# A 2-D Fourier filter with a gated MLP on one core: transposes fetched one round ahead, the spectral products cut into chunks, loads in another order

## The chip, the cores and the metric

The kernel runs on one core of a Trainium2 chip. The metric is the device time of one execution in microseconds (us), median of several runs. The core's engines work side by side, each through its own queue in order: PE (TensorE, matrix products into PSUM), DVE (VectorE), ACT (ScalarE), POOL (GpSimd) and SP (SyncE). SP and ACT also issue the DMA transfers. PSUM has eight banks, and each tile in it takes a whole one here.

## The reference, cut to what matters

```
xn = layernorm(A_x)                              # 2048 x 576
X  = rfft2(xn);  s = irfft2(X * (w_r + 1j*w_i))  # branch A, 2048 x 289 spectrum
z  = gelu(xn @ w_in)                             # branch B, 2048 x 4608
z1 = z[..., :2304];  z2 = layernorm(z[..., 2304:])
g  = silu(((w_sp @ z2 + b_sp) * z1) @ w_out)
return A_x + s * g
```

## The kernel before

Tokens lie in 16 blocks of 128 partitions. The work has these stages.

**Phase 0** (lines 170 to 203) loads x in four pieces, and for each block does the layer norm on DVE and ACT and five transposes on PE. Each transpose goes to one of two PSUM buffers (pool `p0ps`); DVE (L200) and ACT (L202) in turn copy it out into `xnT`.

**The loads** (L247 to L263) are issued in turn on SP and ACT: `WIN2` (weights of branch B), the filter weights `A_w_r` and `A_w_i`, then constants: `CDSD` (first Fourier step), `GA` (second), `M16`, `TW`, `H`, `CINV`. All but `WIN2` land in memory that phase 0 holds until its end.

**Two generators** are then interleaved step by step. `pb1_gen` computes the second half of branch B: products (L481), gelu in five operations (L267 to L276), statistics (L486). `pa_gen` is branch A: first step (L285, copies L289 and L291), second step (L297 to L303), transposes of the filter (L324), then

- *stage B* (L337 to L356): 37 rounds, called `lq`. A round has two transposes into a pool of two buffers (L338), their copies to `tt` (L340, L342), two products each into `pxr` and `pxi` (L345 to L348; one buffer each), and their copies (L349, L350) to the spectrum `Xv`;
- *the filter product* (L359 to L364): six DVE operations over all 4736 columns;
- *stage IB* (L371 to L376): 10 chunks of 512 columns (the last 128), four products and two copies each;
- *the twiddle* (L385 to L390): again six DVE operations over 4736 columns;
- *stage IC* (L398 to L412): 37 rounds built as in stage B, with `dtt`, `pvr`, `pvi`;
- *stage VT* (L431 to L444): 96 transposes through two buffers, copied by L434 and L436, and after each 16 a strided copy (L442, L444), six in all;
- *stage I2* (L457 to L466): the last inverse step, written out to memory.

When `pb1_gen` has ended, the rest of `pa_gen` runs alone. After it the big part of branch B (L543 to L576) and the output (L585 to L608) follow; they use the memory that branch A gives back.

`nc.any` leaves the engine of a copy to a scheduler, which also sets the order of the instructions on each engine by priority and its own estimates. So the order is read from the built program. The large buffers are shared: G0, G1 and the two halves of G23 each hold several of the arrays in turn.

Of the kernel before, what the change touches and what calls it, by code (L numbers as in the profile page):

```python
# [103 lines left out]
def kernel(  # L104
# [173 lines left out]
    def pa_gen():  # L278
        with tc.tile_pool(name="psA", bufs=2, space=bass.MemoryType.PSUM) as psA, \
                tc.tile_pool(name="psA2", bufs=1, space=bass.MemoryType.PSUM) as psA2:  # L280
            for s2 in range(MT):
# [47 lines left out]
                if lq % 10 == 9:  # L329
                    yield  # L330
        yield
        with tc.tile_pool(name="psB", bufs=2, space=bass.MemoryType.PSUM) as psB, \
                tc.tile_pool(name="psB2", bufs=1, space=bass.MemoryType.PSUM) as psB2:
            for lq in range(LQ):
                tt = pas.tile([P, 2, P], BF16, tag="tt")
                for c in range(2):
                    pt = psB.tile([P, P], BF16, tag="tr")  # L337
# [1 line left out]
                    if c == 0:
                        nc.any.tensor_copy(out=tt[:, c, :], in_=pt[:])  # L340
                    else:
                        nc.any.tensor_copy(out=tt[:, c, :], in_=pt[:])  # L342
# [17 lines left out]
        nc.vector.tensor_tensor(out=T2, in0=Xf[:, 1, :], in1=Wf[:, 1, :], op=ALU.mult)  # L360
        nc.vector.tensor_tensor(out=CXv[:, 0, :], in0=T1, in1=T2, op=ALU.subtract)
        nc.vector.tensor_tensor(out=T1, in0=Xf[:, 0, :], in1=Wf[:, 1, :], op=ALU.mult)
        nc.vector.tensor_tensor(out=T2, in0=Xf[:, 1, :], in1=Wf[:, 0, :], op=ALU.mult)
        nc.vector.tensor_tensor(out=CXv[:, 1, :], in0=T1, in1=T2, op=ALU.add)  # L364
        yield
        with tc.tile_pool(name="psIB", bufs=2, space=bass.MemoryType.PSUM) as psIB:
            ch = [(o_, min(512, FD - o_)) for o_ in range(0, FD, 512)]
            for ci, (c0, cs) in enumerate(ch):
                pdr = psIB.tile([P, 512], F32, tag="dr")
                pdi = psIB.tile([P, 512], F32, tag="di")  # L370
                nc.tensor.matmul(pdr[:, 0:cs], lhsT=M16[:, 0, :], rhs=CXv[:, 0, c0:c0 + cs], start=True, stop=False)  # L371
                nc.tensor.matmul(pdr[:, 0:cs], lhsT=M16[:, 2, :], rhs=CXv[:, 1, c0:c0 + cs], start=False, stop=True)
                nc.tensor.matmul(pdi[:, 0:cs], lhsT=M16[:, 0, :], rhs=CXv[:, 1, c0:c0 + cs], start=True, stop=False)
                nc.tensor.matmul(pdi[:, 0:cs], lhsT=M16[:, 1, :], rhs=CXv[:, 0, c0:c0 + cs], start=False, stop=True)
# [5 lines left out]
        DD3 = G2.rearrange("p (c a k) -> p c a k", c=2, a=LQ)  # L380
        twc = TW[:, 0, :, :].to_broadcast((P, LQ, P))
        tws = TW[:, 1, :, :].to_broadcast((P, LQ, P))
        U1 = G1[:, 0:FD].rearrange("p (a k) -> p a k", a=LQ)
        U2 = G1[:, FD:2 * FD].rearrange("p (a k) -> p a k", a=LQ)
        nc.vector.tensor_tensor(out=U1, in0=DD3[:, 0, :, :], in1=twc, op=ALU.mult)  # L385
        nc.vector.tensor_tensor(out=U2, in0=DD3[:, 1, :, :], in1=tws, op=ALU.mult)
        nc.vector.tensor_tensor(out=Ev[:, 0, :, :], in0=U1, in1=U2, op=ALU.subtract)
        nc.vector.tensor_tensor(out=U1, in0=DD3[:, 0, :, :], in1=tws, op=ALU.mult)
        nc.vector.tensor_tensor(out=U2, in0=DD3[:, 1, :, :], in1=twc, op=ALU.mult)
        nc.vector.tensor_tensor(out=Ev[:, 1, :, :], in0=U1, in1=U2, op=ALU.add)  # L390
        yield
        with tc.tile_pool(name="psIC", bufs=2, space=bass.MemoryType.PSUM) as psIC, \
                tc.tile_pool(name="psIC2", bufs=1, space=bass.MemoryType.PSUM) as psIC2:
            for lq in range(LQ):
                dtt = pas.tile([P, 2, P], BF16, tag="dt")
                for c in range(2):
                    pt = psIC.tile([P, P], BF16, tag="tr")
                    nc.tensor.transpose(pt[:], Ev[:, c, lq, :], ident[:])  # L398
                    if c == 0:
                        nc.any.tensor_copy(out=dtt[:, c, :], in_=pt[:])  # L400
                    else:
                        nc.any.tensor_copy(out=dtt[:, c, :], in_=pt[:])
# [237 lines left out]
```

## Time and profile before

| | us |
|---|---|
| median of 6 runs (787.08 to 789.89) | 788.0 |
| the profiled execution | 787.72 |
| its span, first to last instruction | 785.6 |
| PE, DVE, ACT busy | 668.3, 520.5, 336.6 |

The span is 2.1 us shorter than the time of the same execution. Busy shares are means over stages that have different limits, so the profile is best read stage by stage: first the busy time of each engine in each stretch, then what each waits for there. PEclk is the granted clock of TensorE: 1.00 is the level of 2.4 GHz, 0.50 that of 1.2 GHz.

### The profile page before, as it was taken

What the parts mean: (1) busy time and instruction counts of PE and PEld (TensorE: products, weight loads), DVE (VectorE), ACT (ScalarE), POOL (GpSimd) and SP (SyncE); (2) the same over time, 40 slices, a digit from 0 to 9 for tenths busy, and PEclk for the clock granted to TensorE, in tenths of its full rate; (3) what the DMA queues carried; (4) which work ended last, traced back from release to release, by engine and by line L of the source; (5) the groups of instructions that cost most, each with busy time, mean ns of one, the idle gap of its engine ahead of it and who ended that gap; (6) DMA issues with size and microseconds to landing.
All of it is one profiled execution on the core that took longest, in us unless ns stands there. A gap on an engine that the chain in (4) does not pass through costs nothing.

```text
span 785.6 us, 10455 instructions
## 1 busy us (share of the span) xinstructions
PE 668.3 (85%) x3580; PEld 340.4 (43%) x3638; DVE 520.5 (66%) x1499; ACT 336.6 (43%) x891; POOL 15.8 (2%) x32
## 2 busy tenths in 40 slices
PE   2549998787892389687999999999999999989997
PEld 1215664343560156334444444444444444434553
DVE  6756999899738932321797777777777777652232
ACT  3435788787871267764322222222222222212322
POOL 2000000000000011000000000000000000000000
PEclk9988999898655755569899999999999999998999
DMA  7081111111399000003421211111111111015332
GB/s 256 0 297 62 61 62 61 60 61 61 93 189 207 1 1 2 0 31 123 94 47 36 54 43 34 36 39 36 37 35 35 35 35 28 1 49 185 107 92 68
DMA packets 104309, 54.07 MB, mean 69 GB/s; under 512 B 84096, under 2 KB 101120, under 8 KB 104128
## 3 DMA queue, kind: packets, MB, share of 16 engines
q10 hardware_dynamic: 61008, 28.54, 12.8%
q1 hardware_dynamic: 43248, 24.86, 11.7%
q8 instruction: 28, 0.46, 0.2%
q14 instruction: 25, 0.20, 0.1%
HBM read 30.85 MB, written 14.16 MB: 57 GB/s over the span
## 4 chain that ended last, share of the span: by engine, by line
PE 68%; DVE 15%; ACT 9%; DMA 5%; issue 3%; ACTq 0%; DVEq 0%
PE pg L567 32%; PE ph L557 10%; PE py L596 9%; PE ph L481 3%; PE py L457 3%; DVE stats L486 3%; DMA CDSD<-c_cdsd 2%; PE pt L197 2%; DVE zrow L276 2%; DVE x2t L269 2%; DVE ut L273 2%; ACT sg L275 2%; PE pt L431 2%; ACT G L434 2%; PE pvr L406 1%
## 5 line engine op out<-in xcount | busy, mean ns | idle before, releaser
L567 PE MATMUL pg<-WSPT,z2t 128*128 128x512 bf16 x1127 | 252.4, 379 | 1.4
L267 ACT ACTIVATE hs<-ph 128x512 bf16<-128x512 f32 (+1 forms) x152 | 86.0, 576 | 208.4 <-PE ph L557 183.5
L567 PEld LDWEIGHTS <-z2t 128*128 128x128 bf16 x1152 | 112.7, 98 | 135.9
L275 ACT ACTIVATE sg<-ut 128x512 bf16<-128x512 bf16 (+1 forms) x152 | 90.1, 607 | 57.1 <-DVE ut L273 34.1
L481 PE MATMUL ph<-WIN,xnT 128*128 128x512 bf16 (+1 forms) x387 | 95.8, 382 | 5.3 <-ACT hs L267 3.5
L557 PE MATMUL ph<-xnT,wb 128*128 128x512 bf16 x355 | 84.6, 387 | 4.9 <-DMA wb<-in_B_w_in_dram 4.7
L269 DVE TENSOR_TENSOR x2t<-hs 128x512 bf16<-128x512 bf16 (+1 forms) x152 | 60.1, 400 | 41.5 <-ACT hs L267 41.3
L573 DVE TENSOR_TENSOR BUF<-pg,z1T 128x512 bf16<-128x512 f32 x72 | 49.4, 687 | 44.5 <-PE pg L567 43.7
L596 PE MATMUL py<-WOUT,BUF 128*128 128x512 bf16 (+1 forms) x566 | 73.3, 290 | 4.6 <-DMA WOUT<-in_B_w_out_dram 4.0
L550 DVE TENSOR_SCALAR z2t<-z2t,RSTD,NMR 128x128 bf16<-128x128 bf16 x288 | 73.9, 311 | 2.3 <-DMA z2t<-z2n_d 1.9
L273 DVE TENSOR_TENSOR ut<-x2t,hs 128x512 bf16<-128x512 bf16 (+1 forms) x152 | 59.6, 402 | 0.2
L481 PEld LDWEIGHTS <-xnT 128*128 128x128 bf16 x400 | 40.0, 103 | 43.5 <-issue 17.0
L557 PEld LDWEIGHTS <-wb 128*128 128x128 bf16 x360 | 35.7, 99 | 48.8 <-issue 7.6
L596 PEld LDWEIGHTS <-BUF 128*128 128x128 bf16 x576 | 37.5, 99 | 40.7 <-issue 8.0
L486 DVE BATCH_NORM_STATS2 stats<-zrow 128x6 f32<-128x384 bf16 x96 | 49.0, 546 | 0.1
L602 DVE TENSOR_TENSOR g<-hx,sgm 128x576 bf16<-128x576 bf16 x16 | 7.3, 458 | 56.0 <-ACT sgm L600 44.2
L599 ACT ACTIVATE hx<-py 128x512 bf16<-128x512 f32 (+1 forms) x32 | 13.2, 414 | 67.6 <-PE py L596 67.6
L270 DVE TENSOR_SCALAR x2t<-x2t 128x512 bf16<-128x512 bf16 (+1 forms) x152 | 40.6, 278 | 1.0
L197 PE MATMUL pt<-ident,xn 128*128 128x128 bf16 (+1 forms) x80 | 17.9, 281 | 22.9 <-DVE xn L192 10.6
L276 DVE TENSOR_TENSOR zrow<-hs,sg 128x512 bf16<-128x512 bf16 (+1 forms) x80 | 30.0, 388 | 5.3 <-ACT sg L275 5.1
L285 PE MATMUL pf<-CDSD,xnT 128*128 128x296 bf16 x160 | 23.7, 293 | 11.2 <-DMA CDSD<-c_cdsd 9.8
L276 DVE TENSOR_TENSOR z1T<-hs,sg 128x512 bf16<-128x512 bf16 x72 | 30.0, 418 | 1.9 <-ACT sg L275 1.5
(133 smaller groups left out, 727.5 us busy)
## 6 DMA issues: line engine op xcount, KB each, us to landing
z2t<-z2n_d ACTq DMA_DIRECT2D x18, 512.0 KB, 4.0
z2n_d<-zrow ACTq DMA_DIRECT2D x8, 576.0 KB, 2.8
z2n_d<-zrow SPq DMA_DIRECT2D x8, 576.0 KB, 2.8
sspec_d<-srow ACTq DMA_DIRECT2D x16, 144.0 KB, 1.8
wb<-in_B_w_in_dram ACTq DMA_DIRECT2D x72, 32.0 KB, 1.9
GA<-c_ga SPq DMA_DIRECT2D x1, 1536.0 KB, 13.6
WOUT<-in_B_w_out_dram SPq DMA_DIRECT2D x9, 144.0 KB, 3.6
WOUT<-in_B_w_out_dram ACTq DMA_DIRECT2D x9, 144.0 KB, 4.1
```

Of the source, the lines that this page charges most:

```text
L267: nc.scalar.activation(out=hs[:, 0:nsz], in_=ph[:, 0:nsz], func=ACT.Identity)
L269: nc.vector.tensor_tensor(out=x2t[:, 0:nsz], in0=hs[:, 0:nsz], in1=hs[:, 0:nsz], op=ALU.mult)
L273: nc.vector.tensor_tensor(out=ut[:, 0:nsz], in0=x2t[:, 0:nsz], in1=hs[:, 0:nsz], op=ALU.mult)
L275: nc.scalar.activation(out=sg[:, 0:nsz], in_=ut[:, 0:nsz], func=ACT.Sigmoid, scale=GELU_S2)
L276: nc.vector.tensor_tensor(out=dst, in0=hs[:, 0:nsz], in1=sg[:, 0:nsz], op=ALU.mult)
L481: nc.tensor.matmul(ph[:, 0:nsz], lhsT=xnT[:, ks, m * P:(m + 1) * P], rhs=WIN2[:, ks, f0:f0 + nsz], start=(ks == 0), stop=(ks == DKS - 1))
L486: nc.vector.bn_stats(out=stats2[:, ci, :], in_=zrow[:, c0:c0 + cs])
L550: nc.vector.tensor_scalar(out=z2t[:, m, :], in0=z2t[:, m, :], scalar1=RSTD2[:, m, :], scalar2=NMR2[:, m, :], op0=ALU.mult, op1=ALU.add)
L557: nc.tensor.matmul(ph[:, 0:nsz], lhsT=wb[:, ks, :], rhs=xnT[:, ks, nb * 512: nb * 512 + nsz], start=(ks == 0), stop=(ks == DKS - 1))
L567: nc.tensor.matmul(pg[:, 0:nsz], lhsT=z2t[:, ks, :], rhs=WSPT[:, ks, nb * 512: nb * 512 + nsz], start=(ks == 0), stop=(ks == MT - 1))
L573: nc.vector.tensor_tensor(out=dst, in0=pg[:, 0:nsz].rearrange("p (a u) -> p a u", u=P), in1=z1T[:, nb * 512: nb * 512 + nsz].rearrange("p ...
L596: nc.tensor.matmul(py[:, 0:dn], lhsT=BUF[:, m, fi * P:(fi + 1) * P], rhs=WOUT[:, fi, d0:d0 + dn], start=(fi == 0), stop=(fi == FT - 1))
```

## The change

- **Phase 0:** four PSUM buffers for the transposes in place of two, and x in eight pieces in place of four.
- **Loads:** in the text, `CDSD` and `GA` come ahead of `WIN2`; the filter weights come last.
- **First step:** for the first six blocks both copies are put on ACT; the others are left to the scheduler.
- **Stages B and IC:** the transposes of the next round are written ahead of the products of this one, and the transposes' pool has three buffers in place of two.
- **Filter product and twiddle:** each is cut into the 10 chunks. All chunks of the filter product are written ahead of stage IB; the twiddle of a chunk follows the products of that chunk.
- **Stage VT:** four buffers in place of two.

```diff
-            tc.tile_pool(name="p0ps", bufs=2, space=bass.MemoryType.PSUM) as p0ps:
+            tc.tile_pool(name="p0ps", bufs=4, space=bass.MemoryType.PSUM) as p0ps:
...
-        mchunk = max(1, MT // 4)
+        mchunk = max(1, MT // 8)
...
-    for ks in range(DKS):
-        kw = kws[ks]
-        dq().dma_start(out=WIN2[0:kw, ks, :], in_=B_w_in[ks * P: ks * P + kw, Fh:F])
-    dq().dma_start(out=WNv[:, 0, :, 0:Df], in_=A_w_r.rearrange("(k2 k1) l -> k1 k2 l", k1=P))
-    dq().dma_start(out=WNv[:, 1, :, 0:Df], in_=A_w_i.rearrange("(k2 k1) l -> k1 k2 l", k1=P))
...
     dq().dma_start(out=GA[:], in_=cd_ga.ap().rearrange("p (s c k) -> p s c k", s=MT, c=3))
+    for ks in range(DKS):
+        kw = kws[ks]
+        dq().dma_start(out=WIN2[0:kw, ks, :], in_=B_w_in[ks * P: ks * P + kw, Fh:F])
...
     dq().dma_start(out=CINV[:], in_=cd_cinv.ap().rearrange("p (a c d) -> p a c d", a=LCH, c=2))
+    dq().dma_start(out=WNv[:, 0, :, 0:Df], in_=A_w_r.rearrange("(k2 k1) l -> k1 k2 l", k1=P))
+    dq().dma_start(out=WNv[:, 1, :, 0:Df], in_=A_w_i.rearrange("(k2 k1) l -> k1 k2 l", k1=P))
...
-                    if c == 0:
-                        nc.any.tensor_copy(out=Av[:, s2, c, :], in_=pf[:])
+                    if s2 < 6:
+                        nc.scalar.activation(out=Av[:, s2, c, :], in_=pf[:], func=ACT.Identity)
...
-        with tc.tile_pool(name="psB", bufs=2, space=bass.MemoryType.PSUM) as psB, \
+        with tc.tile_pool(name="psB", bufs=3, space=bass.MemoryType.PSUM) as psB, \
...
+            def fwd_tr(lq):
                 tt = pas.tile([P, 2, P], BF16, tag="tt")
...
+            nxt = fwd_tr(0)
+            for lq in range(LQ):
+                tt = nxt
+                if lq + 1 < LQ:
+                    nxt = fwd_tr(lq + 1)
...
-        nc.vector.tensor_tensor(out=T1, in0=Xf[:, 0, :], in1=Wf[:, 0, :], op=ALU.mult)
...
+            for ci, (c0, cs) in enumerate(ch):
+                sl = slice(c0, c0 + cs)
+                T1 = G2[:, c0:c0 + cs]
+                T2 = G2[:, FD + c0:FD + c0 + cs]
+                nc.vector.tensor_tensor(out=T1, in0=Xf[:, 0, sl], in1=Wf[:, 0, sl], op=ALU.mult)
...
+            for ci, (c0, cs) in enumerate(ch):
+                sl = slice(c0, c0 + cs)
                 pdr = psIB.tile([P, 512], F32, tag="dr")
...
+                nc.vector.tensor_tensor(out=U1, in0=D3r, in1=twc, op=ALU.mult)
...
+                nc.vector.tensor_tensor(out=Ei, in0=U1, in1=U2, op=ALU.add)
...
-        with tc.tile_pool(name="psVT", bufs=2, space=bass.MemoryType.PSUM) as psVT:
+        with tc.tile_pool(name="psVT", bufs=4, space=bass.MemoryType.PSUM) as psVT:
```

What the built program makes of it is shown at three places.

**The queues that load, at the end of phase 0.** SP before (G is the memory of the filter weights, WIN that of `WIN2`):

```order
L176 DMA x_all<-in_A_x_dram 128x4x576 x2
L249 DMA WIN_460<-in_B_w_in_dram 128x2304 x2
L249 DMA WIN_460<-in_B_w_in_dram 64x2304
L251 DMA G_450<-in_A_w_i_dram 128x16x289
L255 DMA GA<-c_ga 128x6144
L259 DMA TW<-c_tw 128x256
L263 DMA CINV<-c_cinv 128x3456
```

SP after:

```order
L176 DMA x_all<-in_A_x_dram 128x2x576 x4
L253 DMA WIN_464<-in_B_w_in_dram 128x2304 x2
L253 DMA WIN_464<-in_B_w_in_dram 64x2304
L248 DMA CDSD<-c_cdsd 128x2960
L257 DMA TW<-c_tw 128x256
L261 DMA CINV<-c_cinv 128x3456
L263 DMA G_454<-in_A_w_i_dram 128x16x289
```

`WIN2` stays ahead on both, whatever the text says; `CDSD` goes from ACT to SP, ahead of the filter weights. ACT before, at the same place (hs is the first operation of the gelu):

```order
L202 ACTIVATE xnT<-pt 64x128
L250 DMA G_450<-in_A_w_r_dram 128x16x289
L253 DMA CDSD<-c_cdsd 128x2960
L257 DMA M_473<-c_m 128x384
L261 DMA H<-c_h 128x384
L267 ACTIVATE hs<-ph 128x512 x3
```

ACT after:

```order
L202 ACTIVATE xnT<-pt 64x128
L250 DMA GA<-c_ga 128x6144
L255 DMA M_475<-c_m 128x384
L259 DMA H<-c_h 128x384
L262 DMA G_454<-in_A_w_r_dram 128x16x289
L267 ACTIVATE hs<-ph 128x512 x3
```

ACT still issues four transfers ahead of the first hs, with the filter weights last of them. Each filter weight tensor has 1156 KB. On PE, 30 products of branch B stand ahead of the first one with `CDSD` before, and 15 after, where 10 with `CDSD` follow at once.

**DVE, from stage B to the twiddle.** Before, from the last statistics of `pb1_gen` on:

```order
L487 BN_AGGR MV_70<-stats_2660 128x2
L350 CAST G_448<-pxi 128x128 x28
L359 TENSOR_TENSOR G_450<-G_448,G_450 128x4736
L360 TENSOR_TENSOR G_450<-G_448,G_450 128x4736
L361 TENSOR_TENSOR G_449<-G_450 128x4736
```

After, in the middle of stage B, and then where the filter product ends and the twiddle begins:

```order
L368 TENSOR_TENSOR G_454<-G_452,G_454 128x512
L339 COPY tt<-pt 128x128
L369 TENSOR_TENSOR G_453<-G_454 128x512
L339 COPY tt<-pt 128x128
L370 TENSOR_TENSOR G_454<-G_452,G_454 128x512
```

```order
L372 TENSOR_TENSOR G_453<-G_454 128x512
L368 TENSOR_TENSOR G_454<-G_452,G_454 128x128
L392 TENSOR_TENSOR G_453<-G_454,TW 128x512
L369 TENSOR_TENSOR G_453<-G_454 128x128
L393 TENSOR_TENSOR G_453<-G_454,TW 128x512
```

The filter product now begins within stage B: 18 of its 60 operations stand there one by one between the copies of `tt` that DVE has taken over, the other 42 after them, mixed two chunks at a time; the twiddle follows at once.

**PE, one round of stage B**, with the buffers' numbers (pt a transpose's, tt the round's). Before:

```order
L338 MATMUL pt_2845<-ident_63,G1_449 128x128
L338 LDWEIGHTS G1_449
L338 MATMUL pt_2857<-ident_63,G1_449 128x128
L345 LDWEIGHTS M16_473
L345 MATMUL pxr_2848<-tt_2841,M16_473 128x128
L346 LDWEIGHTS M16_473
L346 MATMUL pxr_2848<-tt_2841,M16_473 128x128
L347 LDWEIGHTS M16_473
L347 MATMUL pxi_2849<-tt_2841,M16_473 128x128
```

After:

```order
L338 MATMUL pt_2819<-ident_63,G1_453 128x128
L338 LDWEIGHTS G1_453
L338 MATMUL pt_2853<-ident_63,G1_453 128x128
L348 LDWEIGHTS M16_475
L348 MATMUL pxr_2807<-tt_2785,M16_475 128x128
L349 LDWEIGHTS M16_475
L349 MATMUL pxr_2807<-tt_2785,M16_475 128x128
L350 LDWEIGHTS M16_475
L350 MATMUL pxi_2808<-tt_2785,M16_475 128x128
```

Before, the first transpose (pt_2845) fills the second half of the very `tt_2841` that the products behind it read. After, both transposes are for later rounds. In stage IC the rows are the same with H, `dtt`, `pvr` and `pvi`.

Copies by engine, counted in the built program: of the 32 of the first step ACT does 30 before and 31 after; in stage IB 12 and 20 of 20; in stage B ACT does 116 before and 124 after, DVE 32 and 24; in stage IC 110 and 136 on ACT, 38 and 12 on DVE; in stage VT 88 and 51 of the 96 on ACT, 8 and 45 on DVE; of the six strided copies ACT does two before and three after, one of them last in both.

## Rows read from the trace of the kernel before

**Rows 1.** Busy time of each engine by stretch; first row names the columns.

```profile
core 0: us, PE busy (x) PEld busy (x) DVE busy (x) ACT busy (x) POOL busy (x), PEclk, DMA share, GB/s
0.00:41.20 41.20, 17.90 (x81) 7.97 (x82) 29.09 (x137) 16.29 (x57) 4.53 (x8) 1.00 0.35 122
41.20:63.60 22.40, 10.83 (x39) 4.67 (x40) 9.30 (x28) 6.88 (x13) 0.00 (x0) 0.79 0.79 262
63.60:209.60 146.00, 124.70 (x704) 74.04 (x715) 136.55 (x432) 117.90 (x300) 0.55 (x2) 0.93 0.16 63
209.60:235.90 26.30, 24.61 (x167) 17.28 (x164) 8.19 (x29) 19.45 (x84) 0.00 (x0) 0.50 0.94 178
235.90:252.00 16.10, 0.79 (x2) 0.39 (x4) 15.74 (x7) 0.08 (x1) 0.00 (x0) 0.50 1.00 204
252.00:261.40 9.40, 9.40 (x38) 3.88 (x36) 4.99 (x8) 5.86 (x11) 0.00 (x0) 0.80 0.39 84
261.40:278.00 16.60, 0.98 (x5) 0.37 (x5) 16.02 (x7) 0.76 (x5) 2.89 (x2) 0.64 0.00 0
278.00:312.50 34.50, 32.33 (x220) 23.19 (x220) 10.55 (x38) 25.42 (x109) 4.31 (x3) 0.50 0.00 1
312.50:343.00 30.50, 20.52 (x96) 9.84 (x94) 9.40 (x13) 22.57 (x90) 0.00 (x0) 0.50 0.00 1
```

**Rows 2.** Waits in phase 0 (5 to 41 us): in total, times, longest.

```profile
ACT xnT L202 <- PE pt L197: 15.6, 38, 0.6
...
PE pt L197 <- ACT xnT L202: 10.3, 26, 1.2
...
DVE stats L186 <- DMA x_all<-in_A_x_dram: 4.7, 1, 4.7
```

**Rows 3.** Timeline, 41 to 61 us: start, length, engine, line, [idle before].

```profile
41.44 3.76 ACTq L253 DMA_DIRECT2D CDSD<-c_cdsd  x1
...
46.89 1.58 ACT L267 ACTIVATE hs<-ph 128x512 bf16<-128x512 f32 x3 [5.78 <-PE ph L481]
...
51.38 0.74 DVE L276 TENSOR_TENSOR zrow<-hs,sg 128x512 bf16<-128x512 bf16 x2
...
60.20 1.18 PE L285 MATMUL pf<-CDSD,xnT 128*128 128x296 bf16 x4 [9.79 <-DMA CDSD<-c_cdsd]
```

**Rows 4.** DMA issues: KB and us from issue to landing.

```profile
CDSD<-c_cdsd ACTq DMA_DIRECT2D x1, 740.0 KB, 18.6
```

**Rows 5.** Timeline, one round of stage B out of 27 alike.

```profile
219.09 0.27 ACT L342 COPY tt<-pt 128x128 bf16<-128x128 bf16 x1
219.25 0.27 ACT L340 COPY tt<-pt 128x128 bf16<-128x128 bf16 x1
219.41 0.27 PE L346 MATMUL pxr<-tt,M 128*128 128x128 bf16 x1
...
219.71 0.27 ACT L349 CAST G<-pxr 128x128 bf16<-128x128 f32 x1 [0.19 <-PE pxr L346]
```

**Rows 6.** Timeline, filter product, second and third of six.

```profile
238.62 2.62 DVE L360 TENSOR_TENSOR G<-G,G 128x4736 bf16<-128x4736 bf16 x1
241.27 2.62 DVE L361 TENSOR_TENSOR G<-G 128x4736 bf16<-128x4736 bf16 x1
```

**Rows 7.** Timeline, stage VT: two of 48 pairs, and a strided copy.

```profile
313.57 0.43 PE L431 MATMUL pt<-ident,G 128*128 128x128 bf16 x2 [0.19 <-ACT G L434]
...
314.04 0.27 ACT L436 COPY G<-pt 128x128 bf16<-128x128 bf16 x1
314.19 0.43 PE L431 MATMUL pt<-ident,G 128*128 128x128 bf16 x2 [0.19 <-ACT G L434]
...
317.43 3.66 ACT L442 COPY G<-G 128x2048 bf16<-128x2048 bf16 x1
```

**Rows 8.** Timeline, stage B among products of branch B, at clock 1.00.

```profile
199.60 0.22 PE L348 MATMUL pxi<-tt,M 128*128 128x128 bf16 x1
```

More of the change, by code (lines that the diff above doesn't have):

```diff
@@ L331, in pa_gen @@
         yield
-        with tc.tile_pool(name="psB", bufs=2, space=bass.MemoryType.PSUM) as psB, \
+        with tc.tile_pool(name="psB", bufs=3, space=bass.MemoryType.PSUM) as psB, \
                 tc.tile_pool(name="psB2", bufs=1, space=bass.MemoryType.PSUM) as psB2:
-            for lq in range(LQ):
+            def fwd_tr(lq):
                 tt = pas.tile([P, 2, P], BF16, tag="tt")
@@ L338, in pa_gen @@
                     nc.tensor.transpose(pt[:], BPv[:, c, lq, :, :], ident[:])
[L339 to L342, printed above, removed]
+                    nc.any.tensor_copy(out=tt[:, c, :], in_=pt[:])
+                return tt
+            nxt = fwd_tr(0)
[3 more added lines that the diff above has]
+                    nxt = fwd_tr(lq + 1)
                 pxr = psB2.tile([P, P], F32, tag="xr")
@@ L356, in pa_gen @@
         FD = LQ * P
-        T1 = G2[:, 0:FD]
-        T2 = G2[:, FD:2 * FD]
-        nc.vector.tensor_tensor(out=T1, in0=Xf[:, 0, :], in1=Wf[:, 0, :], op=ALU.mult)
[L360 to L363, printed above, removed]
@@ L364, in pa_gen @@
-        nc.vector.tensor_tensor(out=CXv[:, 1, :], in0=T1, in1=T2, op=ALU.add)
-        yield
+        Ef = G3.rearrange("p (c f) -> p c f", c=2)
+        ch = [(o_, min(512, FD - o_)) for o_ in range(0, FD, 512)]
         with tc.tile_pool(name="psIB", bufs=2, space=bass.MemoryType.PSUM) as psIB:
-            ch = [(o_, min(512, FD - o_)) for o_ in range(0, FD, 512)]
             for ci, (c0, cs) in enumerate(ch):
+                sl = slice(c0, c0 + cs)
+                T1 = G2[:, c0:c0 + cs]
+                T2 = G2[:, FD + c0:FD + c0 + cs]
+                nc.vector.tensor_tensor(out=T1, in0=Xf[:, 0, sl], in1=Wf[:, 0, sl], op=ALU.mult)
+                nc.vector.tensor_tensor(out=T2, in0=Xf[:, 1, sl], in1=Wf[:, 1, sl], op=ALU.mult)
+                nc.vector.tensor_tensor(out=CXv[:, 0, sl], in0=T1, in1=T2, op=ALU.subtract)
+                nc.vector.tensor_tensor(out=T1, in0=Xf[:, 0, sl], in1=Wf[:, 1, sl], op=ALU.mult)
+                nc.vector.tensor_tensor(out=T2, in0=Xf[:, 1, sl], in1=Wf[:, 0, sl], op=ALU.mult)
+                nc.vector.tensor_tensor(out=CXv[:, 1, sl], in0=T1, in1=T2, op=ALU.add)
+            for ci, (c0, cs) in enumerate(ch):
+                sl = slice(c0, c0 + cs)
@@ L369, in pa_gen @@
                 pdr = psIB.tile([P, 512], F32, tag="dr")
                 pdi = psIB.tile([P, 512], F32, tag="di")
[L371 to L374, printed above, removed]
@@ L375, in pa_gen @@
-                nc.any.tensor_copy(out=DDv[:, 0, c0:c0 + cs], in_=pdr[:, 0:cs])
-                nc.any.tensor_copy(out=DDv[:, 1, c0:c0 + cs], in_=pdi[:, 0:cs])
-                if ci % 5 == 4:
+                nc.tensor.matmul(pdr[:, 0:cs], lhsT=M16[:, 0, :], rhs=CXv[:, 0, sl], start=True, stop=False)
+                nc.tensor.matmul(pdr[:, 0:cs], lhsT=M16[:, 2, :], rhs=CXv[:, 1, sl], start=False, stop=True)
+                nc.tensor.matmul(pdi[:, 0:cs], lhsT=M16[:, 0, :], rhs=CXv[:, 1, sl], start=True, stop=False)
@@ new lines, in pa_gen @@
+                nc.tensor.matmul(pdi[:, 0:cs], lhsT=M16[:, 1, :], rhs=CXv[:, 0, sl], start=False, stop=True)
+                nc.any.tensor_copy(out=DDv[:, 0, sl], in_=pdr[:, 0:cs])
+                nc.any.tensor_copy(out=DDv[:, 1, sl], in_=pdi[:, 0:cs])
+                nlq = cs // P
+                D3r = DDv[:, 0, sl].rearrange("p (a k) -> p a k", a=nlq)
+                D3i = DDv[:, 1, sl].rearrange("p (a k) -> p a k", a=nlq)
+                twc = TW[:, 0, :, :].to_broadcast((P, nlq, P))
+                tws = TW[:, 1, :, :].to_broadcast((P, nlq, P))
@@ new lines, in pa_gen @@
+                U1 = G1[:, c0:c0 + cs].rearrange("p (a k) -> p a k", a=nlq)
+                U2 = G1[:, FD + c0:FD + c0 + cs].rearrange("p (a k) -> p a k", a=nlq)
+                Er = Ef[:, 0, sl].rearrange("p (a k) -> p a k", a=nlq)
+                Ei = Ef[:, 1, sl].rearrange("p (a k) -> p a k", a=nlq)
+                nc.vector.tensor_tensor(out=U1, in0=D3r, in1=twc, op=ALU.mult)
+                nc.vector.tensor_tensor(out=U2, in0=D3i, in1=tws, op=ALU.mult)
+                nc.vector.tensor_tensor(out=Er, in0=U1, in1=U2, op=ALU.subtract)
@@ L378, in pa_gen @@
+                nc.vector.tensor_tensor(out=U1, in0=D3r, in1=tws, op=ALU.mult)
+                nc.vector.tensor_tensor(out=U2, in0=D3i, in1=twc, op=ALU.mult)
+                nc.vector.tensor_tensor(out=Ei, in0=U1, in1=U2, op=ALU.add)
+                if ci % 3 == 2:
                     yield
         yield
[L380 to L390, printed above, removed]
@@ L391, in pa_gen, with inv_tr @@
-        yield
-        with tc.tile_pool(name="psIC", bufs=2, space=bass.MemoryType.PSUM) as psIC, \
+        with tc.tile_pool(name="psIC", bufs=3, space=bass.MemoryType.PSUM) as psIC, \
                 tc.tile_pool(name="psIC2", bufs=1, space=bass.MemoryType.PSUM) as psIC2:
-            for lq in range(LQ):
+            def inv_tr(lq):
                 dtt = pas.tile([P, 2, P], BF16, tag="dt")
@@ L398, in pa_gen @@
                     nc.tensor.transpose(pt[:], Ev[:, c, lq, :], ident[:])
[L399 to L402, printed above, removed]
+                    nc.any.tensor_copy(out=dtt[:, c, :], in_=pt[:])
+                return dtt
+            nxt = inv_tr(0)
+            for lq in range(LQ):
+                dtt = nxt
+                if lq + 1 < LQ:
+                    nxt = inv_tr(lq + 1)
                 pvr = psIC2.tile([P, P], F32, tag="vr")
```

## The prediction

> **What bounds the kernel now.** The first view to read is the busy time by stretch [rows 1], since the mean shares hide that each stage has another limit. The reader is to look, in each row, for the engine whose busy time fills the stretch. From 63.6 to 209.6 us it is DVE (136.6 of 146). Around that stand stretches in which none is full, or one works while the others stand. Phase 0 (to 41.2) has DVE busy for 29.1. From 41.2 to 63.6 DVE is busy for 9.3 of 22.4. In the filter product (235.9 to 252) and the twiddle (261.4 to 278) DVE works alone and PE does next to nothing. Stages B and IC show PE busy almost throughout, but that is the length of operations that wait for each other, at the lower clock, and stage VT has 20.5 of 30.5. After 343 PE is the limit, at the upper clock, and the change touches nothing there.
>
> The waits come next. In phase 0, ACT waits for the transposes 38 times and PE for ACT's copies 26 times, each under 1.3 us [rows 2]: two buffers in a ping-pong. The gap up to 60.2 is a DMA: the first product with `CDSD` waits 9.8 us for it [rows 3], 18.6 us after its issue [rows 4]. One round of stage B shows its own chain [rows 5]: copy L342 (0.27), product L346 0.05 behind it (0.27), copy L349 0.03 behind that (0.27), and 0.05 later the next L342. These make 0.94, which is the period: 26.3 us are 28 rounds.
>
> Everything from 209.6 to 370 is one line of stages, and branch B's big part needs the memory that branch A frees. What these stages lose, the end loses.
>
> **The change, part by part.** The sum is made against the profiled execution, 787.7 us, which is 0.3 below the median.
>
> *Phase 0.* Four buffers take the ping-pong away; DVE's 29.1 us of work stay [rows 1], behind a first wait of 4.7 for x [rows 2]. The floor is then 33.8 against 41.2, so at most 7.4, plus up to 2.4 (half of the first wait) for smaller pieces of x. At worst nothing: DVE's copies now stand in groups that wait for PE. I take **4**, between the ends (0 to 9).
>
> *Loads.* The built order leaves `WIN2` first on both queues, so branch B's first products don't suffer. `CDSD` now stands first on SP behind `WIN2` and shares the transfers with `GA` alone. Its 740 KB and as much of `GA` take 5.6 us at the 262 GB/s of that stretch [rows 1, 4]; I reckon 7 us after phase 0 against 18.8. PE has 15 products of branch B ahead of it. What counts is DVE's idle time there: 13.1 us now. The first hs comes 5.7 us after phase 0's end now [rows 3], because ACT issues four transfers ahead of it; of these the filter weights went behind, `GA` came in. I reckon 4 for that and 3 for the gap behind `CDSD`: 7 idle instead of 13.1, so **6** (2 if ACT's issue costs as much as now and `CDSD` lands at 12; 10 at best). The later filter weights cost nothing: their first user stands behind both Fourier steps, well inside the stretch that DVE fills, and that covers them (without it they would cost at most their own time, some 9 us for 2.3 MB at 262 GB/s). The ACT copies of the first step cost nothing either: ACT had 30 of these 32 before.
>
> *Stage B.* The transposes are for a later round, so L342 and its hand-over (0.32) leave the chain. What stays is the single `pxr` buffer: first product to second, the second's 0.27, 0.03, the copy's 0.27, 0.05. With 0.16 for the first (two transposes 0.43 less one product 0.27 [rows 5, 7]) that is 0.78; without it, 0.62. I take 0.75, near the upper end, as each product pair must wait for its buffer. DVE now has a filter operation and a `tt` copy in each such round, 0.37 (half of the 0.74 for two of that size [rows 3]) and 0.27 if it costs what it does on ACT [rows 5], which fits in 0.75 but tightly. 28 rounds by 0.19: **5.3** (0 if DVE holds the copies back, 9 at 0.62).
>
> Here the clock matters. The row of stage B shows 0.50, the level of 1.2 GHz, through all of it [rows 1], with PE counted busy for 24.6 of 26.3. The Trainium skill ("TensorE: Matmul & The Clock Gate", section "What's actually happening") says that the slow level is the default and that activity releases it. By the trace, 94% counted busy did not release it here; a denser round might. With the clock of this stage kept, the sum stands; the other way is a rival below.
>
> *Filter product, stage IB, twiddle.* Now 42.1 us lie between the end of B (235.9) and the start of IC (278). The product's operations are dense: 2.65 apart for 4736 columns [rows 6], 0.37 for 512; by these two an operation of 128 columns is an estimated 0.16. So the 60 of them grow from 15.7 us to some 21. But 18 are done between the copies of B, and in the 9 rounds after these (7 us) another 18. That leaves 18 by 0.37 and 6 by 0.16 at B's end, 7.7 us, and 8 operations more until the first twiddled chunk: 10.6. Stage IB can start at once on the first chunks. All 20 of its copies are on ACT now, 0.5 apart (three such in 1.58 [rows 3]): 9.4, plus some 2.6 for the first chunk at the lower clock, 12. IC needs the banks of IB, so it starts 12.5 after B. The rest of the twiddle (21 us in all) ends 29 after B, under IC, which lasts to 40. Gain 42.1 less 12.5: **29.6**. At best IB takes its present 9.4 and the gain is 32. At worst each DVE operation costs 0.74, as if none overlapped: then 33 are left at B's end and IC starts some 28 later, gain 13.
>
> *Stage IC.* As in B: 37 rounds by 0.19, **7**. ACT has 3.7 copies a round here, 0.16 apart when they come one behind another [rows 5], 0.6 a round. If each cost its full 0.27 the round would be 1.0 and the stage 2 us slower; at 0.62, 12 faster.
>
> *Stage VT.* Now 44 pairs on ACT, 0.62 each [rows 7], and two strided copies of 3.66: 34.6 us, of which the last copy runs on beyond 343. Four buffers and both engines: ACT has 51 by 0.16 and three strided copies, 19.1 us, and this is its floor. PE waits in order for both engines, so a strided copy on either stops the other after four buffers; I take 23, **11.5** less (4 to 15).
>
> The sum is 4 + 6 + 5.3 + 29.6 + 7 + 11.5 = 63.4; 787.7 less 63.4 is 724.3, against the median **725**.
>
> **The rivals.**
>
> *The clock rises in B and IC.* By the rule above. A 128-column product took 0.22 at the upper clock [rows 8] against 0.27, so two of them in the chain make the round 0.65: 65 rounds by 0.1, 6.5 less, 718. For it: the two products of the chain come denser, and in stage IB the clock rose within the stretch (0.80) [rows 1]. Against it: 0.50 throughout B, IC and VT.
>
> *The overlap is half lost.* DVE takes its instructions in order, and a `tt` copy behind a filter operation that waits for the one before it holds PE. Take 0.55 an operation (midway between 0.37 and 0.74): B gains nothing, 29 operations are left at its end, IC starts 19 after (gain 23), IC gains 2: 46.5 in all, 741. For it: the three operations in a group depend on each other. Against it: from the third chunk on two chunks alternate.
>
> *Slower: small operations on DVE become the line.* If the 120 chunked operations cost so much that they set the end from 209.6 to IC's end, the stretch is 120 p plus some 3 us for the last rounds. Now it is 102.9, and the loads, phase 0 and VT give 21.5 more; slower begins at p over 1.02 us, and at 1.1 the time is 797. The nearest row has 0.37 [rows 3], so p would have to be nearly three times that.
>
> *The change doesn't do what it says.* For the loads this is half so (`WIN2` stays first) and is in the sum. For the stages the built order shows the moves, so only a wait that the order doesn't name could undo them, and that is the second rival.
>
> **How the numbers follow.** Forecast 725: 0.67. Clock 718: 0.15. Overlap half lost 741: 0.15. Slower: 0.03. The single bounds, if they don't all fall on one side, leave about 12 us either way around 725; to take in both rivals the range is 708 to 745. A measurement of this kernel can tell 0.2%, or 1.6 us, from no change. All cases but one lie far on the fast side: faster 0.96, same 0.01, slower 0.03.
>
> **What would show it.** In the profile after: the first `pf` product no later than 10 us behind the end of phase 0, and phase 0 ending at 37. In B and IC one round every 0.75 us, with the copy of `tt` no longer in front of the product. No stretch where DVE is full and PE empty; filter operations between B's copies, twiddle operations beside stage IB and IC, and 12 us from the last copy of B to the first transpose of IC. VT in 23 us with DVE's copies beside ACT's. The part after it unchanged, to a microsecond. Wrong would be: PE waiting for `tt` copies on DVE, ACT full in IC with rounds over 0.9, gaps behind strided copies in VT as long as the copies themselves, or DVE's statistics in the long stretch ending later than its shift.

## The result, and the profile after

| | before | after |
|---|---|---|
| median, us | 787.9 (16 runs) | 712.5 (8 runs, 711.5 to 713.3) |
| ratio | 1 | 0.904 (0.903 to 0.905) |
| span of the profiled execution, us | 785.6 | 710.1 |

The forecast was 725, with a range of 708 to 745. The time came out 12.5 us below the forecast, in the range, and 5.5 below the rival in which the clock rises (718).

The busy time by stretch, cut at the ends of the stages. The columns are those of [rows 1], and the stretches are phase 0, the loads, the long stretch with branch B, stage B, the gap up to IC's first transpose, IC, VT and I2:

```profile
core 0: us, PE busy (x) PEld busy (x) DVE busy (x) ACT busy (x) POOL busy (x), PEclk, DMA share, GB/s
0.00:35.90 35.90, 14.11 (x80) 7.64 (x81) 28.45 (x137) 15.21 (x57) 4.53 (x8) 1.00 0.42 140
35.90:50.00 14.10, 12.90 (x56) 6.69 (x58) 7.56 (x24) 8.07 (x16) 0.00 (x0) 1.00 0.98 337
50.00:194.40 144.40, 122.07 (x695) 72.62 (x705) 137.68 (x438) 118.11 (x304) 0.42 (x2) 0.93 0.19 71
194.40:211.60 17.20, 16.56 (x158) 11.99 (x157) 15.86 (x56) 16.62 (x86) 0.00 (x0) 1.00 0.96 186
211.60:221.90 10.30, 8.67 (x39) 3.79 (x40) 10.30 (x36) 9.54 (x22) 0.00 (x0) 1.00 0.99 199
221.90:247.30 25.40, 23.52 (x222) 17.04 (x222) 18.57 (x63) 24.42 (x136) 7.19 (x4) 1.00 0.77 143
247.30:268.40 21.10, 14.74 (x96) 9.45 (x96) 13.47 (x48) 17.66 (x55) 0.00 (x0) 0.54 0.00 0
268.40:294.50 26.10, 25.52 (x188) 12.69 (x192) 3.91 (x16) 12.40 (x17) 0.00 (x0) 0.91 0.25 85
```

The reader is to see three things. The two stretches in which DVE worked and PE stood [rows 1] are gone: between B and IC lie 10.3 us, in which PE, DVE and ACT all work. The clock is 1.00 in B and IC, where it was 0.50. And in IC another engine is full now, ACT with 24.4 of 25.4. One number of the first two rows misleads: they print a clock of 1.00, but the products L493 of 512 columns start 0.43 us apart until 40.7 us and 0.22 apart from 41 us on, so PE ran slower there at first. In the kernel before, L481 changes in the same way at 44 us.

The gains by stage, from the ends of the stages in both traces (the long stretch up to the end of its last statistics, VT up to I2's first product):

| | predicted | from the two traces |
|---|---|---|
| phase 0 | 4 | 5.1 |
| loads and the long stretch | 6 | 10.3 |
| stage B | 5.3 | 8.8 |
| filter product, IB, twiddle | 29.6 | 31.8 |
| stage IC | 7 | 9.1 |
| stage VT | 11.5 | 9.5 |
| rest | 0 | 0.9 |
| sum | 63.4 | 75.5 |

The timeline behind phase 0 (start, length, engine, line) answers to [rows 3] and [rows 4]:

```profile
35.73 0.34 SPq L248 DMA_DIRECT2D CDSD<-c_cdsd  x1
...
38.62 0.60 ACT L267 ACTIVATE hs<-ph 128x512 bf16<-128x512 f32 x1 [2.61 <-PE ph L493]
...
41.63 1.42 PE L285 MATMUL pf<-CDSD,xnT 128*128 128x296 bf16 x10
```

The first hs comes 2.7 us behind phase 0 (5.7 before), and the first product with `CDSD` waits for nothing.

One round of stage B, which answers to [rows 5]; then one of IC:

```profile
202.87 0.27 ACT L352 CAST G<-pxr 128x128 bf16<-128x128 f32 x1
...
203.17 0.23 DVE L339 COPY tt<-pt 128x128 bf16<-128x128 bf16 x1
203.19 0.22 PE L348 MATMUL pxr<-tt,M 128*128 128x128 bf16 x1
...
203.25 0.22 PE L349 MATMUL pxr<-tt,M 128*128 128x128 bf16 x1
203.31 0.41 DVE L368 TENSOR_TENSOR G<-G,G 128x512 bf16<-128x512 bf16 x1
203.50 0.27 ACT L352 CAST G<-pxr 128x128 bf16<-128x128 f32 x1
```

```profile
231.87 0.32 ACT L423 CAST G<-pvr 128x128 bf16<-128x128 f32 x1
...
232.04 0.32 ACT L424 CAST G<-pvi 128x128 bf16<-128x128 f32 x1
232.20 0.50 ACT L408 COPY dtt<-pt 128x128 bf16<-128x128 bf16 x2
...
232.55 0.32 ACT L423 CAST G<-pvr 128x128 bf16<-128x128 f32 x1
```

In B the chain is the copy (0.27), 0.05, 0.06 from the first product to the second, 0.22, 0.03: 0.63. The copy of `tt` has left it. In IC four copies stand on ACT one behind another, each longer than in B (0.32 for 0.27) while DVE computes the twiddle beside them, and the period is 0.68. Behind the twiddle, from 240 us on, DVE takes one of the four copies, those on ACT last 0.27 again, and the round takes 0.62:

```profile
241.45 0.27 ACT L423 CAST G<-pvr 128x128 bf16<-128x128 f32 x1
...
242.08 0.27 ACT L423 CAST G<-pvr 128x128 bf16<-128x128 f32 x1
```

### The profile page after: what moved, and what is told of

Read it like the earlier page. It is cut to its first block, busy times and chain, and to the rows that moved or that the text cites. A ratio compares the mean times of both kernels' runs of the same rounds, so it can differ in the third digit from the quotient of the medians.

```text
span 710.1 us, 10619 instructions
## 1 busy us (share of the span) xinstructions
PE 637.8 (90%) x3580; PEld 327.8 (46%) x3638; DVE 512.5 (72%) x1600; ACT 331.0 (47%) x898; POOL 15.6 (2%) x32
## 4 chain that ended last, share of the span: by engine, by line
PE 67%; DVE 15%; ACT 13%; DMA 2%; issue 2%; ACTq 0%; DVEq 0%
PE pg L579 35%; PE ph L569 11%; PE py L608 9%; PE ph L493 4%; PE py L469 4%; DVE stats L498 4%; DVE zrow L276 2%; ACT sg L275 2%; DVE ut L273 2%; DVE x2t L269 2%; ACT dtt L408 2%; DMA WOUT<-in_B_w_out_dram 1%; ACT tt L339 1%; PE pf L285 1%; DVE stats L186 1%
## 5 line engine op out<-in xcount | busy, mean ns | idle before, releaser
L493 PE MATMUL ph<-WIN,xnT 128*128 128x512 bf16 (+1 forms) x387 | 95.1, 382 | 5.0 <-ACT hs L267 3.7
L493 PEld LDWEIGHTS <-xnT 128*128 128x128 bf16 x400 | 40.1, 103 | 42.8 <-issue 17.2
L611 ACT ACTIVATE hx<-py 128x512 bf16<-128x512 f32 (+1 forms) x32 | 13.2, 414 | 66.7 <-PE py L608 46.1
L197 PE MATMUL pt<-ident,xn 128*128 128x128 bf16 (+1 forms) x80 | 14.1, 296 | 21.6 <-DVE xn L192 19.1
L588 DVE TENSOR_TENSOR BUF<-BUF,zb 128x512 bf16<-128x512 bf16 x72 | 28.9, 420 | 1.3
```

The source lines that it names most:

```text
L493: nc.tensor.matmul(ph[:, 0:nsz], lhsT=xnT[:, ks, m * P:(m + 1) * P], rhs=WIN2[:, ks, f0:f0 + nsz], start=(ks == 0), stop=(ks == DKS - 1))
```

## The experiments

All times are medians, and all ratios are against the kernel before, which was measured again beside them; its medians there were 786.8 to 787.8, so differences of about a microsecond between runs say nothing. The first six experiments undo one part of the change each (reference 712.5, ratio 0.904).

### Phase 0 undone

```
-  p0ps bufs=4, mchunk = MT // 8
+  p0ps bufs=2, mchunk = MT // 4
```

> The changed kernel with phase 0 as before (two PSUM buffers, x in four pieces), all else kept. Theory (the parts add up): phase 0 ends at 41 us again in place of 35.9, everything behind it is shifted by the same 5.2 us, time 717.7. Rival (the loads hide it): DVE stood idle for 6.5 us behind phase 0 in the changed kernel, and part of the 5.2 goes into that gap, time 713 to 715.

Measured: 718.2 (0.9125, 0.911 to 0.914), 5.7 more. Phase 0 ends at 41.1 and everything behind is shifted. PE waits for ACT's copies as before [rows 2]; in the changed kernel these waits are 0.6 us in all:

```profile
PE pt L197 <- ACT xnT L202: 10.3, 26, 1.2
```

So the gain is mainly the ping-pong's, and the idle time behind phase 0 hides none of it. The run undoes the buffers and the pieces of x together. The smaller pieces let DVE's first statistics start 1.1 us earlier (its first wait is 3.6 for 4.7), but the first transpose only 0.2; up to 1.1 us can be theirs.

### Loads undone

```
-  CDSD, GA, WIN2, M16, TW, H, CINV, filter weights
+  WIN2, filter weights, CDSD, GA, M16, TW, H, CINV
```

> The changed kernel with the loads written in the old order (WIN2 and the filter weights ahead of CDSD and GA), all else kept; PE's order puts 30 products of branch B ahead of the first with CDSD again. Theory (the whole of the 10 us by which the long stretch came out shorter lies in the loads): CDSD lands some 18 us behind phase 0, DVE waits 6 to 7 us for the first hs and once more some 7 us behind the products with CDSD, time 722 to 723. Rival (the loads are worth the predicted 6, the other 4 come from the copies of the first step on ACT): time 718.5.

Measured: 723.3 (0.919, 0.918 to 0.921), 10.8 more. So the whole 10.3 lies in this edit. DVE's waits in the 30.8 us behind phase 0 (us, times, longest) show the size:

```profile
DVE x2t L269 <- ACT hs L267: 14.1, 2, 8.1
```

There are two long waits, one for the first hs and one for the next group of hs behind the products that wait for `CDSD`. In the changed kernel this wait is 5.1 in all.

### The first step's copies left to the scheduler

```
-  if s2 < 6: nc.scalar.activation(out=Av[...], in_=pf[:])
-  else: nc.any.tensor_copy(...)
+  nc.any.tensor_copy(out=Av[...], in_=pf[:])
```

> The changed kernel with the copies of the first step left to the scheduler for all blocks, all else kept; the scheduler still puts 31 or more of 32 on ACT or splits them, but PE's order changes: 45 products with CDSD stand in one piece ahead of the second group of branch B, where the changed kernel has 10. Theory of the prediction (the engine of these copies costs nothing): 712.5. Rival (the edit acts through PE's order): 35 products more without branch B's, at 0.15 us, keep DVE waiting for some 5 us near the start, time 716 to 718.

Measured: 715.6 (0.9095, 0.908 to 0.911), 3.1 more, just under the rival's range; in the trace, whose execution took 716.6, the long stretch ends 5.1 us later. The rival's time was nearly met, its reason was not: the scheduler also puts 12 of the 32 copies on DVE, where the changed kernel has one. DVE's group of that line (count, busy us, mean ns, idle before):

```profile
L288 DVE CAST G<-pf 128x296 bf16<-128x296 f32 x12 | 5.6, 467 | 8.8 <-ACT hs L267 7.0 <-PE pf L285 1.8
```

That is 5.1 us more than the one copy takes. Other copies move between DVE and ACT too, so DVE's busy time from 36 us to the end of the stretch grows by 3.9 (145.3 to 149.1), and its idle time by 1.2 (13.2 to 14.4). The two together are the 5.1; of the waiting of some 5 us that the rival expected, 1.2 is there.

### Filter product and twiddle over whole columns

The 120 chunked operations are replaced by the 12 of before; the rounds of B and IC stay.

> The changed kernel with the filter product and the twiddle as six operations over all 4736 columns each, as before; stages B and IC keep their transposes one round ahead. Theory (the parts add up): 40 to 42 us between the last copy of B and the first transpose of IC in place of 10.3, rounds of B and IC at the upper clock and 0.60 to 0.63 us, time 742 to 744. Rival (DVE's chunk operations held the rounds up): the rounds without them are clearly shorter, 0.55, time 737 or less. Of the clock: if the rounds themselves hold it up, it is 1.00 in B; after 15 us without PE it may start low in IC.

Measured: 743.9 (0.945, 0.944 to 0.947), 31.4 more, as the sum of parts wants. B lasts as long without the chunk operations (17.8 us), so these don't hold its rounds up. IC gives what the prediction lacked, the same rounds at both clocks. The windows name stretch, busy times and clock; then copy L419 of successive rounds at 0.50 and at 1.00:

```profile
245.70:248.00 2.30, 0.53 (x2) 0.11 (x2) 2.30 (x1) 0.27 (x1) 0.00 (x0) 0.50 0.00 0
...
256.00:258.00 2.00, 2.00 (x18) 1.69 (x17) 0.87 (x4) 1.87 (x9) 0.00 (x0) 0.50 0.00 0
258.00:260.00 2.00, 1.97 (x18) 1.46 (x17) 1.09 (x5) 1.46 (x7) 0.00 (x0) 0.74 0.00 0
260.00:262.00 2.00, 1.80 (x20) 1.39 (x20) 0.71 (x4) 1.84 (x11) 0.00 (x0) 1.00 0.01 4
```

```profile
254.69 0.27 ACT L419 CAST G<-pvi 128x128 bf16<-128x128 f32 x1
...
255.41 0.27 ACT L419 CAST G<-pvi 128x128 bf16<-128x128 f32 x1
```

```profile
264.49 0.27 ACT L419 CAST G<-pvi 128x128 bf16<-128x128 f32 x1
...
265.11 0.27 ACT L419 CAST G<-pvi 128x128 bf16<-128x128 f32 x1
```

The period is 0.72 at the lower clock and 0.62 at the upper. The clock rises at 259 us, when PE has run six of these rounds and nothing between them; in the kernel before, the old rounds ran at 0.50 through all of IC, 34.5 us [rows 1]. So the round with its transposes one ahead is what raises it here.

### The rounds undone

The loops of B and IC are those of before (transposes in the round, two buffers); the chunks stay.

> The changed kernel with the loops of stages B and IC as before (transposes within the round, two buffers), the chunks kept. Theory (the clock rose because the rounds became denser): the clock is 0.50 in B and IC again and the period 0.94, 28 rounds by 0.32 and 37 by 0.26 make 18.6 more, time 731. Rival (the clock rose because DVE's chunks keep the stages going without a hole in front of IB and IC): the clock stays at 1.00 and only the chain's longer copy remains, period about 0.87, 14 us more, time 726.

Measured: 724.4 (0.919, 0.918 to 0.921), 11.9 more: below both expectations. In B and IC the windows show:

```profile
195.40:205.00 9.60, 9.40 (x83) 7.36 (x83) 7.78 (x28) 8.57 (x41) 0.00 (x0) 0.76 0.87 154
205.00:214.60 9.60, 8.98 (x82) 6.44 (x81) 9.29 (x30) 9.20 (x50) 0.00 (x0) 1.00 1.15 204
...
224.60:243.00 18.40, 15.93 (x112) 11.26 (x112) 15.19 (x48) 14.91 (x74) 0.00 (x0) 0.57 0.83 172
243.00:261.00 18.00, 16.51 (x111) 11.51 (x109) 5.49 (x21) 13.13 (x57) 7.09 (x4) 0.50 0.00 1
```

IC does what the theory says: the clock falls to 0.50, a round takes 0.94 to 1.00, and the stage lasts 36.4 us against 25.6. B does not: it lasts 19.2 against 17.5, and its clock rises at 200 us. Here are a window ahead of that, and copy L349 of `pxr` in successive rounds:

```profile
196.50:199.50 3.00, 3.00 (x26) 2.57 (x25) 2.45 (x9) 2.56 (x12) 0.00 (x0) 0.50 0.43 98
```

```profile
197.54 0.27 ACT L349 CAST G<-pxr 128x128 bf16<-128x128 f32 x1
...
198.27 0.29 DVE L349 CAST G<-pxr 128x128 bf16<-128x128 f32 x1 [0.20 <-PE pxr L346]
...
199.02 0.27 ACT L349 CAST G<-pxr 128x128 bf16<-128x128 f32 x1
```

DVE has some of the copies of `tt` and `pxr`, so copies that stood one behind another on ACT [rows 5] run side by side. This brings the old round from 0.94 to 0.74 while the clock is still 0.50; then the clock rises, and the round takes 0.64. As in the whole-column run, shorter rounds come first and the clock follows. In B the old loop beside the chunks gets most of the gain; in IC only the rounds ahead, with their third buffer, bring it.

### Stage VT with two buffers

```
-  psVT bufs=4
+  psVT bufs=2
```

> The changed kernel with two PSUM buffers in stage VT, all else kept; the scheduler then puts 90 of the 96 copies on ACT and five of the six strided copies on DVE. Theory (the gain of VT comes from the buffers and from DVE as a second taker): pairs 0.62 apart again, 45 of them 28 us and a strided copy at the end, VT in 28 to 31 us in place of 21.1, time 720 to 722. Rival (the strided copies set VT's length, and they are faster on DVE): time 713 to 716.

Measured: 719.3 (0.913, 0.912 to 0.915), 6.8 more, a little under the theory. Pairs are 0.62 apart again, and VT takes 29.5 us against 20.9 from transpose to I2's first product; 1.7 of the difference are transposes that start earlier, beside IC. The buffers and the copies on DVE changed together, so their shares aren't parted. The scheduler's split shows the price of a strided copy on each engine (ns min/median/max, starts):

```profile
L454 DVE COPY G<-G x3: 1890/1898/1903, 249.7 to 264.6; 128x2048 bf16<-128x2048 bf16 x2, 40x2048 bf16<-40x2048 bf16 x1
...
L454 ACT COPY G<-G x1: 3678/3678/3678, 274.5 to 274.5; 40x2048 bf16<-40x2048 bf16 x1
```

ACT needs 3.68 us where DVE needs 1.90.

### More work on PE in the kernel before

```
+  pj = psF.tile([P, 256], F32)
+  nc.tensor.matmul(pj, lhsT=M16[:, 2, :], rhs=...)   # every round of B, IC with H
```

> The kernel before with one more product of 256 columns in every round of stages B and IC, into a bank of its own that nothing reads: it adds work to PE off the chain of the round. Theory (a denser PE raises the clock, and the clock shortens the round): the granted clock rises above 0.50 in B and IC, the one product in the chain takes 0.22 in place of 0.27, period 0.88 to 0.90 in place of 0.94, time 784 to 786, faster although work was added. Rival (the clock in these stages is not set by what PE does): it stays at 0.50, the filler of some 0.2 us fits in the round or lengthens it, time 788 to 795.

Measured: 791.9 (1.0045, 1.003 to 1.006), clock 0.50 in the rounds. This run tells nothing of the question: its filler read `xnT`, which is there from the start, and the trace has none of these products in the rounds; the scheduler had moved them ahead, into the long stretch, which ends 4.5 us later. That the time lies in the rival's range is therefore luck. The next run binds them to the round.

> The kernel before, again with one more product of 256 columns in every round of stages B and IC, now reading the round's own tt or dtt, so that it can't be moved out of the round (in the first try the scheduler had put them elsewhere); nothing reads its result. In PE's order it stands ahead of the next round's transposes. Theory (a denser PE raises the clock, and the clock shortens the round): the granted clock rises above 0.50 in B and IC, the filler takes 0.1, the product in the chain 0.22 in place of 0.27, period 0.87 to 0.90 in place of 0.94, time 783 to 786. Rival (what raised the clock in the changed kernel is not how dense PE is): it stays at 0.50, the filler puts 0.2 in front of the transposes, period 1.1 to 1.15, 65 rounds, time 798 to 801.

Measured: 787.6 (1.002, 0.999 to 1.005), no difference in the median, and the two stages of the profiled execution (787.1) say why. Copy L352 in B, then L417 in IC:

```profile
226.24 0.27 ACT L352 CAST G<-pxr 128x128 bf16<-128x128 f32 x1 [0.30 <-PE pxr L347]
...
227.13 0.27 ACT L352 CAST G<-pxr 128x128 bf16<-128x128 f32 x1 [0.30 <-PE pxr L347]
```

```profile
288.09 0.27 ACT L417 CAST G<-pvr 128x128 bf16<-128x128 f32 x1 [0.35 <-PE pvr L410]
...
289.28 0.27 ACT L417 CAST G<-pvr 128x128 bf16<-128x128 f32 x1 [0.35 <-PE pvr L410]
```

In B the clock is 1.00 from 211 us on, the round takes 0.89, and the stage ends after 23.6 us in place of 26.3 with more work in it. In IC the clock stays at 0.50 from 277 to 295 us, the round takes 1.19, and then it rises and the round takes 0.89 there too. So more work on PE does raise the clock, and the clock does shorten the round; but in IC, from the lower level, the rise took 18 us, and what B gained IC lost. The ten executions differ in this: eight took 785.5 to 789.5 at a mean clock of 0.921 to 0.931, two took 795.5 and 795.8 at 0.911 and 0.907. All ten lie above the 0.887 to 0.893 of the kernel before beside them, so the higher clock is not one execution's chance.

### Versions that go on from there

First, VT inside I2: for each of the 16 token groups six transposes go into one bank, then come two copies in place of six and the group's 12 products; there are no strided copies.

> The changed kernel with stage VT put inside stage I2: for each of 16 token groups six transposes into one PSUM bank, two copies (512 and 256 columns) in place of six, then that group's 12 products; no strided copies, the rows are written to memory with a stride. Theory (VT is bound by copies, I2 by PE): a group takes PE 1.6 us of products and 0.6 of transposes, 16 groups 35 to 37 us in place of 47.2, time 701 to 703. Rival (the copies of 512 columns between transposes and products, or the clock, stall PE): 2.9 us a group, time 712.

Measured: 712.3 (0.904, 0.903 to 0.906), no gain. PE is full at clock 1.00, and its 12 products take 2.37 us, while weight loads come late around those with 40 rows:

```profile
272.92 2.37 PE L457 MATMUL py<-CINV,G 128*128 128x512 bf16 x12
...
273.45 0.09 PEld L457 LDWEIGHTS <-G 40*128 40x128 bf16 x1 [0.42 <-issue]
...
273.77 0.11 PEld L457 LDWEIGHTS <-G 128*128 128x128 bf16 x2 [0.23 <-issue]
```

The next version lets all products read 128 rows (the added rows meet zeros in `CINV`).

```
-  lhsT=VTs[0:lsz, m, j, :], rhs=CINV[0:lsz, lc, c, ...]
+  lhsT=VTs[:, m, j, :], rhs=CINV[:, lc, c, ...]
```

> The version with stage VT inside I2, where all six products of a sum now read 128 rows; in the version before two of six read 40 rows, and the weight loads around those came 0.42 and 0.23 us late. Theory (the change between products of 40 and of 128 rows costs the lost time): the 12 products of a group take 1.63 us as in I2 of the changed kernel in place of 2.37, a group 2.25, 16 groups 36 us and 2 at the start, in place of 47.2, time 702 to 704. Rival (the products are slow because the group's copies and transposes stand between them): a group stays at 2.8 to 2.9, time 712.

Measured: 697.0 (0.885, 0.884 to 0.887), 15.3 less than the version with 40 rows. The same 12 products, which now do more arithmetic:

```profile
266.03 1.64 PE L457 MATMUL py<-CINV,G 128*128 128x512 bf16 x12
```

A group takes 2.02, less than the sum of 1.64 and 0.6, whose ends overlap.

Then one copy for two tiles in B and IC, and in phase 0:

```
-  pt[P, P] twice, copied to tt[:, 0], tt[:, 1];  pxr, pxi copied apart
+  pt[P, 2, P], one copy to tt;  px[P, 2, P] (two in turn), one copy to Xv[:, :, lq]
```

> The last version, and in stages B and IC the two transposes of a round share one PSUM bank and one copy of 256 columns, and so do its two sums (two such banks in turn). Theory (in IC the round is bound by ACT, busy for 24.4 of 25.4 us with four copies of 128 columns a round): two copies of 256 cost 0.54 where four of 128 cost 0.64, rounds of 0.55, 4 to 6 us less than the version without it, time 697 to 699. Rival (the round is bound by the hand-over from product to copy to the next product, which gets longer when one copy waits for four products): rounds of 0.65 or more, time 703 or above.

Measured: 691.4 (0.878, 0.876 to 0.880), 5.6 less. A round of IC takes 0.56 in place of 0.68, and ACT is busy throughout in both versions (10.0 of 10 us beside the twiddle): two copies 0.28 apart in place of four 0.17 apart. So ACT's copies bind it in both. What the second pair of banks for the sums brings is not parted from this.

> The version with merged copies, and in phase 0 the five transposes of a block share one PSUM bank: ACT copies the four full ones at once (512 columns), DVE the fifth (64 rows). Theory (phase 0 is now bound by DVE's own work, 28.5 of 35.9 us): 24 of DVE's 40 copies of 0.22 go, 5.3 us, and part of its 2.2 us of waits for the transposes; phase 0 ends 4 to 6 us earlier, time 686 to 687. Rival (it is bound by the hand-over of the statistics between DVE and ACT, which the longer copy on ACT stands in the way of): no gain, 691 or slower.

Measured: 687.5 (0.8725, 0.871 to 0.874), 3.9 less than without it, a little under the expected gain. DVE's busy time in phase 0 falls from 28.5 to 23.9. This version is the fastest here: 25 us below the changed kernel.

## Why the prediction was right, and where it was off

The changes did what was forecast of each, in its place, and the gain came out 12 us above the forecast sum. Of these 12 the rounds of B and IC have 5.6, the loads 4.3, the filter product and twiddle 2.2, phase 0 1.1 and the rest 0.9; VT came out 2 below its term and hides that much of the others. Term by term:

*Phase 0: right, mis-sized by 1.1.* It ends at 35.9, not 37. The undone run gives 5.7, for the buffers and the smaller pieces of x together.

*Loads: mis-sized, 10.3 to 10.8 for 6.* The failed step is "what counts is DVE's idle time there: 13.1 us now". It was read from a stretch that ended at 63.6, in the middle of a wait. Behind it a second wait for hs, 7.25 us long, ended only at 64.2, and one of 1.9 for sg followed. Over the 30.8 us behind phase 0 DVE was busy for 15.0 before and for 24.2 after: 9.2, nearly all of the gain. The 7 us of idle time that were to be left came true: 6.6.

*"The ACT copies of the first step cost nothing either: ACT had 30 of these 32 before": wrong step, no harm.* The comparison was with the old order. With `CDSD` early the scheduler would have put 12 on DVE; without the edit DVE has 3.9 us more work and 1.2 more of waiting in the long stretch (3.1 in the median of the time).

*Stage B and IC: mechanism right, clock wrong.* The transposes left the chain, and the single `pxr` buffer is what stays. At the lower clock the round is 0.72, where the prediction had 0.75. But "With the clock of this stage kept, the sum stands" did not come true; the rival did, whose argument was that a denser round might release the clock. In IC of the whole-column run, where only rounds of the new form run on PE, the clock is 0.50 at the start and 1.00 after some of them. The Trainium skill, "TensorE: Matmul & The Clock Gate", section "What's actually happening", says that activity releases the slow level. This trace agrees. The 0.50 throughout B and IC before, which I held against the rival, was itself a product of the old rounds: they keep it in IC of the run with the rounds undone. In B the round came out at 0.62 to 0.63 (rival: 0.65). In IC it was 0.68 beside the twiddle. The step that failed there is ACT's "0.6 a round": ACT had all four copies, 0.17 apart, and so became the bound; in the last rounds, where DVE takes one of the four, the round is 0.62. Per round in B, some 0.2 of the gain is the shorter chain (0.94 to 0.72 at the lower clock) and 0.1 the clock (0.72 to 0.62).

*Filter product, IB, twiddle: right.* 10.3 us lie between the last copy of B and the first transpose of IC, forecast 12.5; the 2.6 us for a first chunk at the lower clock were not needed. The rival in which half the overlap is lost fell: chunk operations don't slow B's rounds (whole-column run). So did the one in which they become the line: it needs over 1.02 us an operation, and those of 512 columns start 0.34 apart behind B. (At 1.1 us its sum gives 798, not 797.)

*VT: mis-sized, 9.5 for 11.5.* The prediction compared 23 with 34.6, in which the last strided copy is counted, though it runs beside I2. Counted from the start of the stretch to the end of that copy, VT is 24.8 against 34.3. The 23 was a guess above ACT's floor of 19.1; PE did wait behind strided copies on ACT, twice, for 4.1 us in all.

*Not to be parted:* the five undone parts add up to 66.6 of the 75.4 us, and with the first step's copies 69.7. The rest is shared: in B, which gains 8.8, the chunks without the new rounds keep 7.1 of it and the new rounds without the chunks 8.5.

## What to carry to other kernels

Read idle time from a stretch that ends where no wait runs, or the longest wait is cut in two. Where a round at the lower clock waits for copies, price a shorter chain at both clocks, since the same edit can raise the clock; and after it, count copies by engine, for the next bound is likely there. An edit that leaves the engine to a scheduler is to be compared with what the scheduler would do in the new order, not in the old.

## What the runs showed that was not expected

- A strided copy of 2048 columns took 3.68 us on ACT and 1.90 on DVE.
- Products that read 40 rows among those of 128 made 12 products take 2.37 us; with 128 rows in all of them the 12 took 1.64.
- The same rounds with a filler product ran at either level: in stage B, where the clock was 0.50 only from 207 to 211 us, they took 0.89 at 1.00; in stage IC they took 1.19 at 0.50 for some 18 us (277 to 295). Why the clock took so long to rise there, and why two of ten executions were 8 us longer, isn't settled by these runs.
- Copies on ACT of the same size took 0.32 us beside the chunked twiddle on DVE, and 0.27 behind it and in stage B. What lengthens them was not tested.
